# Second weights loaded in longer runs, features dealt to blocks in another way, order searched anew

## The chip, the cores and the metric

The kernel runs on one core of a Trainium2 chip. The metric is device microseconds of one execution; lower is better. Three executions of the kernel before took 1167.38, 1167.28 and 1159.86 us, with a median of 1167.28 us.

## The reference, cut to what matters

Two layers follow each other. The first is a causal weighted sum of seven neighbouring tokens, with weights from a softmax; its output is the input of the second, a layer of eight experts in which each token goes to one expert.

```python
w = softmax(weight_gen, axis=-1)                        # (8, 3584, 8 heads, 7 taps)
out[b, s, h, :] = sum_k w[b, s, h, k] * x_pad[b, s + k, h, :]   # x: (8, 3584, 192), heads of 24
x = out.reshape(28672, 192)

logits = x @ w_gate                                     # 8 experts
e_idx = argmax(logits); gate_w = softmax(logits)[e_idx]
eom = sigmoid(x @ w_output_gate)
for e in range(8):                                      # w1: (8, 192, 1024), w2: (8, 1024, 192)
    h = relu(x[mask] @ w1[e])
    out[mask] = gate_w * eom[:, e] * (h @ w2[e])
```

## The kernel before, in words

**The front** works on 32 units of 896 tokens (128 partitions by 7 tokens). For a unit, `load_steps` (line 655) loads `x` and the tap weights `w`, `softmax_steps` makes the weights, and `tap_steps` makes seven products of 128x1344. GpSimd makes some of them (the tile `gap`), VectorE the others; how many each makes for unit u is `TAPS(u)` (line 1409), from `PRO_G`, `FIRST_G`, `SHARES` and `POOL`. For the first `PE_U` = 6 units the sum of the seven products is made by TensorE: the first product is written to PSUM and the other six are added by float32 matmuls with the identity matrix `cf`, six instructions to a tap (`add_steps`, line 825). From unit 6 on VectorE adds them (`acc_steps`, line 775). `sum_steps` (line 850) scales a unit, splits it in two halves of float16 (the tile `rt`), and computes the router's logits. For these the unit is turned: for the first `TR_U` = 5 units by 21 TensorE transposes and 7 ScalarE copies to `gt`, afterwards by one transposing DMA on SP's queue (`gt<-rt`). `place_steps` (line 998) gives each token a row in the sorted tensor `srtd` in DRAM, and GpSimd scatters the rows with 7 indirect DMAs a unit (`srtd<-rt,posi`).

**The weights.** `weight_steps` (line 586) loads `w1` (4096- and 2048-byte runs) and `w2` of an expert into staging tiles `st1` and `st2`; four pairs of those exist. `split_steps` (line 603) takes the sum of squares (ScalarE, `sqd`), a scale, and writes each weight as two float16 halves: ScalarE writes the high half, VectorE the low one (`SCALAR_TENSOR_TENSOR`), into `wa` for `w1` and `wpb` for `w2`. Eight DMAs of an expert carry them back to the DRAM tensor `wd`. In `w2`'s load, partition p gets the eight rows p, 128+p, 256+p, ..., each a run of 768 bytes.

**The tiles.** As soon as enough rows are sorted, `plan_rounds` calls for tiles of 256, then 384, then 512 rows of one expert, at the end also of 128; there are 75 of them. `tile_steps` (line 1148) lets the first one go only when all eight experts are in `wd` (`state["weights"] == NE`), and `round_steps` only when the scatters of all units up to its own are issued; the first round is that of unit 2. `tile_load` (line 1170) reads the expert's number, the rows by a transposing DMA (`xT`), and both weights from `wd` (`wa<-wd`, `wb<-wd`), 1.6 MB a tile. `gemm1_unit` (line 1186) makes five matmuls to each block of 128 hidden features; ScalarE and VectorE evacuate them as two float16 halves (`hh`, `hl`). `gemm2_group` (line 1208) makes 24 matmuls of 192 columns to a group of 128 rows; ScalarE scales the result (`ys`), and GpSimd scatters it to the output.

**The order.** The program is written out by hand on all engines: generators ("chains") give up their turn at each `yield`, and `Order.step` always takes the one that its own estimate of times, a rank and a small favour put first. The estimate's constants, ranks, favours, shares and limits stand at the end of the file (from line 1415) and fix the order of the instructions on each engine. `stir` (line 502) puts dummy matmuls on TensorE where the estimate sees a gap (`STIR`). All DMAs but the scatters go out on SP's queue, in order. An instruction that a paced engine issues has line 207 in the profile; a DMA of SP's has line 175.

Of the kernel before, what the change touches and what calls it, by code (L numbers as in the profile page):

```python
# [14 lines left out]
ALU = mybir.AluOpType  # L15
AX = mybir.AxisListType.X

P = 128
# [138 lines left out]
class Queue:  # L157
# [12 lines left out]
    def __getattr__(self, name):  # L170
        f = getattr(self.engine, name)

        def call(*args, **kwargs):
# [6 lines left out]
            if own is not None:  # L180
# [3 lines left out]
                self.moved = max(self.moved, done)  # L184
                c.t = max(c.t, done + LANDED)
            return r
# [4 lines left out]
class Paced:  # L191


    def __init__(self, order, engine, cost, before=0.0, after=None, lead=0.0, follows=True, holds=None, first=None):
        self.order, self.engine, self.cost, self.t = order, engine, cost, 0.0
        self.before, self.after = before, LAT if after is None else after
        self.lead, self.follows, self.holds, self.first = lead, follows, holds, first
# [91 lines left out]
def sync_cost(name, args, kwargs):  # L289
    if not name.startswith("dma_start"):  # L290
        return None
    o = kwargs["out"]
    size = 4 if o.dtype in (F32, I32) else 2
    n = size
    for v in o.shape:
        n *= v
    if name == "dma_start_transpose":
        return n / 256 * 0.0185 / 16
    run = n // o.shape[0]
    if tuple(o.shape[1:]) == (8, 192):  # L300
        run = 768
    per = 0.009 if run <= 64 else 0.0265 + run / 6148 * 0.2145
    return n / run * per / 16

# [2 lines left out]
def kernel(ctx: ExitStack, tc: tile.TileContext, x, wg, wgate, wogate, w1, w2, cst, out):  # L307
    nc = tc.nc
    od = Order()
    V = Paced(od, nc.vector, vector_cost, holds=two_in_sbuf)  # L310
    S = Paced(od, nc.scalar, scalar_cost, after=LAT_S)
    G = Paced(od, nc.gpsimd, gpsimd_cost, holds=lambda kwargs: True)
    T_ = Paced(od, nc.tensor, tensor_cost, after=0.0, first=lambda gap: stir(gap))
    SP = Queue(od, nc.sync, sync_cost, sync_issue, LEAD)
    TQ = SP if TURN_SP else Queue(od, nc.scalar, sync_cost, sync_issue, LEAD, S)
    B, SEQ, D = x.shape
# [153 lines left out]
    o = 256  # L470
# [115 lines left out]
    def weight_steps(stg):  # L586

        for e in range(NE):
            yield from take(st_free, SP)

            st1 = stg.tile([P, 1536], F32, tag="st1", name=f"st1_{e}")
            st2 = stg.tile([P, 1536], F32, tag="st2", name=f"st2_{e}")
            SP.dma_start(out=st1[:, 0:1024], in_=w1[e, 0:128, :])
            for h in range(2):
                SP.dma_start(out=st1[64 * h : 64 * h + 64, 1024:1536], in_=w1[e, 128:192, 512 * h : 512 * h + 512])
            SP.dma_start(out=st2.rearrange("p (c d) -> p c d", d=D), in_=w2[e].rearrange("(c p) d -> p c d", p=P))
            od.add(split_steps(e, st1, st2), (RANK_W, e), S)
            if 3 < e < 7:

                scattered(SP.dma_start(out=srtd[DUMMY + (e - 3) * P : DUMMY + (e - 2) * P, :], in_=pad), -1)  # L600
            od.cur.t = od.now

    def split_steps(e, st1, st2):
        yield from take(sq_free, S)
        sqd = stg_sq.tile([P, 1536], BF16, tag="sqd", bufs=1, name=f"sqd{e}")
        ss = sp.tile([P, 2], F32, tag="wss", name=f"wss{e}")
        S.activation(sqd, st1, AF.Square, accum_out=ss[:, 0:1])
        yield S
        S.activation(sqd, st2, AF.Square, accum_out=ss[:, 1:2])
        sq_free.append(od.cur.t)  # L610
        yield from take(pg_free, T_)
        pg = ps[:, 1984:1986]
        T_.matmul(pg[:, 0:2], lhsT=ones32, rhs=ss, start=True, stop=True)
        yield V
        sc = sp.tile([P, 2], F32, tag="wsc", name=f"wsc{e}")
        inv = sp.tile([P, 2], F32, tag="winv", name=f"winv{e}")
        yield from scales(pg[:, 0:2], sc, inv, f"w{e}", pg_free)
        s1, s2 = sc[:, 0:1], sc[:, 1:2]
        _, wa = yield from take(wa_free, S)
        wah = wa.bitcast(F16)  # L620

        for lo, n in ((0, 1024), (2048, 512)):
            src = st1[:, lo // 2 : lo // 2 + n]
            hi = wah[:, lo : lo + n]
            yield S
            S.activation(hi, src, AF.Copy, scale=s1)
            yield V
            V.scalar_tensor_tensor(out=wah[:, lo + n : lo + 2 * n], in0=src, scalar=s1, in1=hi, op0=ALU.mult, op1=ALU.subtract)
        yield SP
        SP.dma_start(out=wd[e, :, 0:1024], in_=wa[:, 0:1024])  # L630
        for h in range(2):
            for q in range(2):
                SP.dma_start(out=wd[e, 64 * q : 64 * q + 64, 1024 + 256 * h : 1280 + 256 * h], in_=wa[64 * h : 64 * h + 64, 1024:1280])
            SP.dma_start(out=wd[e, 0:64, 1536 + 256 * h : 1792 + 256 * h], in_=wa[64 * h : 64 * h + 64, 1280:1536])
        wa_free.append((od.cur.t, wa))
        od.cur.t = od.now
        yield from take(wb_free, S)
        wb = wp.tile([P, WW - 2048], I32, tag="wb", bufs=WB, name=f"wpb{e}")
        wbh = wb.bitcast(F16)
        hi = wbh[:, 0:1536]  # L640
        yield S
        S.activation(wb.bitcast(F32)[:, 1536:1537], inv[:, 0:1], AF.Copy, scale=inv[:, 1:2])
        S.activation(hi, st2, AF.Copy, scale=s2)
        yield V
        V.scalar_tensor_tensor(out=wbh[:, 1536:3072], in0=st2, scalar=s2, in1=hi, op0=ALU.mult, op1=ALU.subtract)
        st_free.append(od.cur.t)
        yield SP
        SP.dma_start(out=wd[e, :, 2048:WW], in_=wb)
        wb_free.append((od.cur.t, "wb"))
        state["weights"] += 1  # L650
# [199 lines left out]
    def sum_steps(u):  # L850
# [40 lines left out]
        else:  # L891
            od.cur.t += LAT_T
            for j0 in range(0, JS, 2):
# [292 lines left out]
    def gemm1_unit(hp, d, u, at):  # L1186

        t, T, wa, xT = d["t"], d["T"], d["wa"], d["xT"]
        nf = 512 // T
        hh = hp.tile([P, 512], F16, tag="hh", name=f"hh{t}_{u}")  # L1190
        hl = hp.tile([P, 512], F16, tag="hl", name=f"hl{t}_{u}")
        for i in range(nf):
            f = u * nf + i
            b3 = 2048 + f * P
            for q, (wo, k) in enumerate(((f * P, 0), (1024 + f * P, 0), (f * P, 2), (b3, 1), (b3 + 1024, 1))):
                T_.matmul(ps[:, at + i * T : at + (i + 1) * T], lhsT=wa[:, wo : wo + P], rhs=xT[:, k, 0:T], start=(q == 0), stop=(q == 4), skip_group_check=True)
        od.add(evac_steps(d, ps[:, at : at + nf * T], hh[:, 0 : nf * T], hl[:, 0 : nf * T], at, u), (RANK_H,), S, T_.t + LAT_P)
# [10 lines left out]
    def gemm2_group(d, g, at):  # L1208
        t, T, wb = d["t"], d["T"], d["wb"]
        if g == 0:  # L1210
            d["ys"] = gp.tile([P, 4, D], F32, tag="ys", bufs=YB, name=f"ys{t}")
            d["sc"] = gp.tile([P, 4], F32, tag="sc", name=f"sc{t}")
        py = ps[:, at : at + D]
        nf = 512 // T
        for f in range(8):
            lo = (f % nf) * T + g * P
            hh = d["hh"][f // nf][:, lo : lo + P]
            hl = d["hl"][f // nf][:, lo : lo + P]
            w2h = wb[:, f * D : (f + 1) * D]
            w2l = wb[:, 1536 + f * D : 1536 + (f + 1) * D]  # L1220
            T_.matmul(py, lhsT=hh, rhs=w2h, start=(f == 0), stop=False)
            T_.matmul(py, lhsT=hh, rhs=w2l, start=False, stop=False)
            T_.matmul(py, lhsT=hl, rhs=w2h, start=False, stop=(f == 7))
        if g == d["G"] - 1:
            wb_free.append((T_.t + WBX, d["kb"]))
        od.add(out_steps(d, g, py, at), (RANK_Y,), S, T_.t + LAT_P)
# [122 lines left out]
    with tc.tile_pool(name="stg", bufs=STG, reuse_waits="tile") as stg:  # L1349
        stg_sq = stg  # L1350
        od.add(weight_steps(stg), (RANK_W, 0), SP)
        while state["weights"] < NE:
# [26 lines left out]
    with tc.For_i(0, left, 1):  # L1379
# [8 lines left out]
        d = tile_load(state["t"], P, ti, 0, ([], []), more, "wb")  # L1388
# [26 lines left out]
RANK_H, RANK_Y, RANK_C, RANK_R, RANK_B, RANK_A, RANK_G = 1, 0, 2, 3, 4, 5, 6  # L1415
HOLDS = {128: 768, 256: 1408, 384: 2304, 512: 2816}
TAILK = 79
RANK_W = 4.808
LAT = 0.076
LAT_S = 0.2324  # L1420
LAT_P = 0.384
LAT_T = 1.932
LOCK = True
ARRIVE = 1.9478
LANDED = 0.4
LAT_R = 0.851
SLACK = 0
SCATTER = 0.987
SMALL = 0.073
EAGER = 0, 0.2, (2, 3, 4)  # L1430
BACK = 0.899
W_LATE = 0
T_LATE = 0
TURNS = (1536,)
# [3 lines left out]
WB = 4  # L1438
HB = 16
AHEAD = 2  # L1440
DELAY = {128: 5, 256: 2, 384: 1, 512: 1}
LATE = 4
LATE_W = 4
XN = 3
# [3 lines left out]
MB = 8  # L1448
PRO_G = 4
POOL = (5, 5, 5, 4)  # L1450
SHARES = {11: 4, 28: 5, 20: 5, 2: 3, 4: 4, 29: 5, 6: 5, 23: 4, 1: 4, 27: 5, 0: 4, 30: 4, 18: 5, 14: 5, 26: 5, 19: 4, 15: 5, 25: 4, 31: 4, 22: 5, 3: 6}
FAVOUR = {'evac 1 0': 0.3, 'evac 72 6': 0.1, 'evac 1 4': -1.0, 'out 36 0': 0.8, 'evac 73 1': -0.5, 'out 33 1': 1.4}
PE_U = 6
STIR = (0.46, 0.31)
GIVE = 1
RANK_X = 2.767
X_EARLY = 4
RANK_GATE = 4.308
FIRST_G = (5, 4)
DEFER = 4  # L1460
WBX = 3.58
ROW = ()
PAIRS = 0
TURN_SP = True
GT = 1
TR_U = 5
EARLY = {2: ((256, 0),), 4: ((384, 0),), 5: ((384, 0),), 6: ((384, 0),), 3: ((384, 0),)}
EVERY = {*range(99)}
MANUAL = ("SP", "DVE", "PE", "Activation", "Pool")
# [18 lines left out]
```

## Time and profile before

| what | before |
|---|---|
| median of three executions | 1167.28 us |
| the profiled execution | 1169.75 us, of which the span is 1168.0 us |
| TensorE busy | 1096.7 us (94%) |
| VectorE busy | 939.9 us (80%) |
| GpSimd busy | 840.6 us (72%) |
| ScalarE busy | 620.9 us (53%) |
| mean granted TensorE clock | 0.973 |
| DMA packets | 294952, of which 229222 under 512 bytes |

The busy shares are means over two very different stages: until the first tile's matmuls (147.59 us) the kernel prepares weights and the first units, and from then to the end the tiles' matmuls run beside the front. Views by stretch tell the two apart.

### The profile page before, as it was taken

What the parts mean: (1) busy time and instruction counts of PE and PEld (TensorE: products, weight loads), DVE (VectorE), ACT (ScalarE), POOL (GpSimd) and SP (SyncE); (2) the same over time, 40 slices, a digit from 0 to 9 for tenths busy, and PEclk for the clock granted to TensorE, in tenths of its full rate; (3) what the DMA queues carried; (4) which work ended last, traced back from release to release, by engine and by line L of the source; (5) the groups of instructions that cost most, each with busy time, mean ns of one, the idle gap of its engine ahead of it and who ended that gap; (6) DMA issues with size and microseconds to landing.
All of it is one profiled execution on the core that took longest, in us unless ns stands there. A gap on an engine that the chain in (4) does not pass through costs nothing.

```text
span 1168.0 us, 26970 instructions
## 1 busy us (share of the span) xinstructions
PE 1096.7 (94%) x9622; PEld 804.3 (69%) x9622; DVE 939.9 (80%) x1874; ACT 620.9 (53%) x1300; POOL 840.6 (72%) x622
## 2 busy tenths in 40 slices
PE   8978588999999999999999999999999999999997
PEld 4544377777667766677667666767667777788897
DVE  6889879999999989888899999999999863333331
ACT  4986644566555545555555555555545544443442
POOL 7578775888788888788888898888888764322222
PEclk9988888999999999999999999999999999999999
DMA  9997899999996987979997897889958997699993
GB/s 291 275 309 247 247 271 316 280 273 262 249 242 157 246 192 209 250 213 244 230 232 205 255 273 196 237 216 250 254 155 224 231 256 233 189 293 273 299 320 90
DMA packets 294952, 282.77 MB, mean 242 GB/s; under 512 B 229222, under 2 KB 254423, under 8 KB 294816
## 3 DMA queue, kind: packets, MB, share of 16 engines
q1 hardware_dynamic: 272976, 236.54, 76.2%
q0 software_dynamic: 21696, 44.30, 12.5%
q8 instruction: 76, 1.25, 0.5%
q14 instruction: 60, 0.49, 0.1%
q10 hardware_dynamic: 144, 0.20, 0.1%
HBM read 174.77 MB, written 60.28 MB: 201 GB/s over the span
## 4 chain that ended last, share of the span: by engine, by line
PE 44%; DVE 26%; DMA 13%; issue 7%; POOL 6%; ACT 2%; SPq 1%; POOLq 0%; DVEq 0%; ACTq 0%
PE ps L207 44%; DVE ps L207 13%; DVE hl L207 6%; DMA gt<-rt 4%; POOL srtd L207 2%; POOL gap L207 2%; DMA wd<-wa 2%; DMA srtd<-rt,posi 2%; DVE rt L207 2%; DVE vt L207 2%; DMA wa<-wd 2%; POOL out_dram L207 1%; DMA w<-in_wg_dram 1%; SPq L175 1%; ACT rt L207 1%
## 5 line engine op out<-in xcount | busy, mean ns | idle before, releaser
L207 PE MATMUL ps<-xT,wa 128*128 128x512 f16 (+3 forms) x2480 | 503.0, 351 | 27.0 <-DMA wa<-wd 17.1
L207 PE MATMUL ps<-wb,hh 128*128 128x192 f16 x3648 | 473.5, 247 | 3.4 <-DVE hl L207 2.7
L207 PE MATMUL ps<-wb,hl 128*128 128x192 f16 x1824 | 451.0, 247 | 0.0
L207 DVE SCALAR_TENSOR_TENSOR hl<-ps,hh 128x512 f16<-128x512 f32 (+1 forms) x470 | 306.1, 664 | 143.8 <-ACT hh L207 143.4
L207 POOL TENSOR_TENSOR gap<-x,w 128x1344 f32<-128x1344 f32 x147 | 383.6, 2614 | 41.6 <-issue 10.9
L207 PEld LDWEIGHTS <-wa 128*128 128x128 f16 x2480 | 231.8, 99 | 215.8 <-issue 18.8
L207 ACT ACTIVATE hh<-ps 128x512 f16<-128x512 f32 (+1 forms) x470 | 270.5, 582 | 191.0 <-PE ps L207 188.2
L207 PEld LDWEIGHTS <-hh 128*128 128x128 f16 x3648 | 333.0, 98 | 45.0 <-issue 5.3
L207 POOL DMA_INDIRECT out_dram<-ys,meta x220 | 218.8, 995 | 187.3 <-ACT ys L207 141.0
L207 POOL DMA_INDIRECT srtd<-rt,posi x224 | 224.6, 1003 | 85.6 <-issue 60.7
L207 ACT ACTIVATE ys<-ps,sc 128x192 f32<-128x192 f32 x228 | 95.7, 420 | 223.6 <-PE ps L207 155.3
L207 DVE TENSOR_TENSOR ps<-ps,gap 128x1344 f32<-128x1344 f32 x123 | 191.0, 1553 | 3.7 <-POOL gap L207 3.6
L207 PEld LDWEIGHTS <-hl 128*128 128x128 f16 x1824 | 179.4, 98 | 0.1
L207 PE MATMUL ps<-gap,cf 128*128 128x512 f32 x144 | 64.9, 593 | 2.3 <-POOL gap L207 2.3
L207 DVE SCALAR_TENSOR_TENSOR rt<-ps,sx,rt 128x448 f16<-128x448 f32 x64 | 57.5, 909 | 9.5 <-ACT rt L207 7.7
L207 ACT ACTIVATE rt<-ps 128x1344 bf16<-128x1344 f32 x32 | 41.3, 1291 | 22.6 <-DVE ps L207 20.6
L207 ACT ACTIVATE rt<-ps,sx 128x1344 f16<-128x1344 f32 x32 | 44.1, 1377 | 14.7 <-DVE sx L207 14.0
L207 DVE TENSOR_TENSOR ps<-ps,vt 128x1344 f32<-128x1344 f32 x33 | 51.2, 1551 | 0.0
L207 DVE TENSOR_TENSOR vt<-x,ps 128x1344 f32<-128x1344 f32 x33 | 50.9, 1542 | 0.1
L207 DVE TENSOR_TENSOR ps<-x,ps 128x1344 f32<-128x1344 f32 x32 | 49.7, 1552 | 0.6 <-DVE ps L207 0.2
L207 PEld LDWEIGHTS ps<-gap,cf 128*128 128x128 f32 x144 | 27.9, 205 | 29.6 <-issue 25.8
L207 PEld LDWEIGHTS <-gt 128*128 128x128 f16 x672 | 24.3, 97 | 32.8 <-ACT gt L207 13.9
(123 smaller groups left out, 774.5 us busy)
## 6 DMA issues: line engine op xcount, KB each, us to landing
wb<-wd SPq DMA_DIRECT2D x75, 768.5 KB
wa<-wd SPq DMA_DIRECT2D x62, 768.0 KB
x<-in_x_dram SPq DMA_DIRECT2D x32, 672.0 KB
late<-wd SPq DMA_DIRECT2D x13, 768.0 KB
wa<-wd SPq DMA_DIRECT2D x62, 128.0 KB
w<-in_wg_dram SPq DMA_DIRECT2D x32, 196.0 KB
wd<-wpb SPq DMA_DIRECT2D x8, 768.5 KB
st<-in_w_dram SPq DMA_DIRECT2D x8, 768.0 KB
```

The lines of the kernel that those rows point to most:

```text
L175: r = f(*args, **kwargs)
L207: r = f(*args, **kwargs)
```

## The change

The second weights are loaded so that partition p gets, in each half of 512 rows, four neighbouring rows: two runs of 3072 bytes in place of eight of 768. Hidden feature 512h + 4p + c then stands in row p of block (h, c). So that the first product delivers the features in the same blocks, the columns of `w1` are read with a step of four elements when they are split (both ScalarE's and VectorE's read of `st1`); what is written stays contiguous. The two matmul functions index the blocks accordingly. The planner's price of the `w2` load is changed to the longer run. All other edits are constants that fix the order.

```diff
-    if tuple(o.shape[1:]) == (8, 192):
-        run = 768
+    if tuple(o.shape[1:]) == (2, 768):
+        run = 3072
...
-            SP.dma_start(out=st2.rearrange("p (c d) -> p c d", d=D), in_=w2[e].rearrange("(c p) d -> p c d", p=P))
+            SP.dma_start(out=st2.rearrange("p (h n) -> p h n", h=2), in_=w2[e].rearrange("(h p c) d -> p h (c d)", p=P, c=4))
...
-            src = st1[:, lo // 2 : lo // 2 + n]
-            hi = wah[:, lo : lo + n]
+            src = st1[:, lo // 2 : lo // 2 + n].rearrange("p (q c) -> p c q", c=4)
+            hi, low = (wah[:, at : at + n].rearrange("p (c q) -> p c q", c=4) for at in (lo, lo + n))
...
-            V.scalar_tensor_tensor(out=wah[:, lo + n : lo + 2 * n], in0=src, scalar=s1, in1=hi, op0=ALU.mult, op1=ALU.subtract)
+            V.scalar_tensor_tensor(out=low, in0=src, scalar=s1, in1=hi, op0=ALU.mult, op1=ALU.subtract)
...
-            b3 = 2048 + f * P
+            b3 = 2048 + (f % 2 * 4 + f // 2) * P
...
-            w2h = wb[:, f * D : (f + 1) * D]
-            w2l = wb[:, 1536 + f * D : 1536 + (f + 1) * D]
+            row = (f % 2 * 4 + f // 2) * D
+            w2h = wb[:, row : row + D]
+            w2l = wb[:, 1536 + row : 1536 + row + D]
...
-RANK_W = 4.808
+RANK_W = 4.243
...
-BACK = 0.899
+BACK = 1.0
...
-DELAY = {128: 5, 256: 2, 384: 1, 512: 1}
+DELAY = {128: 3, 256: 2, 384: 1, 512: 1}
...
-SHARES = {11: 4, 28: 5, 20: 5, 2: 3, 4: 4, 29: 5, 6: 5, 23: 4, 1: 4, 27: 5, 0: 4, 30: 4, 18: 5, 14: 5, 26: 5, 19: 4, 15: 5, 25: 4, 31: 4, 22: 5, 3: 6}
-FAVOUR = {'evac 1 0': 0.3, 'evac 72 6': 0.1, 'evac 1 4': -1.0, 'out 36 0': 0.8, 'evac 73 1': -0.5, 'out 33 1': 1.4}
-PE_U = 6
-STIR = (0.46, 0.31)
+SHARES = {11: 4, 28: 5, 20: 5, 29: 5, 6: 5, 23: 4, 1: 3, 24: 5, 9: 5, 18: 5, 26: 6, 3: 5, 19: 3, 15: 3, 31: 4, 25: 5, 7: 5, 21: 5, 5: 5, 27: 4, 2: 5, 10: 5}
+FAVOUR = {'place 7': 0.1, 'evac 33 0': 0.4, 'copy 0': -0.8, 'out 68 0': 0.3, 'evac 50 4': 1.4}
+PE_U = 7
+STIR = (1.17, 0.37)
 GIVE = 1
-RANK_X = 2.767
-X_EARLY = 4
-RANK_GATE = 4.308
-FIRST_G = (5, 4)
+RANK_X = 1.564
+X_EARLY = 3
+RANK_GATE = 3.529
+FIRST_G = (4, 4)
 DEFER = 4
-WBX = 3.58
-ROW = ()
+WBX = 2.799
+ROW = (6,)
...
-TR_U = 5
+TR_U = 4
```

Left out are small changes of the estimate's latencies (`LAT`, `LAT_S`, `LAT_T`, `LANDED`, `LAT_R`, `SLACK`). `RANK_W`, `RANK_X` and `RANK_GATE` rank the weights, the early loads (of units up to `X_EARLY`) and the gate's weights against other chains; `DELAY` is the distance between a tile's two products; `WBX` is when a weight buffer counts as free; `ROW` lets a unit's seven scatters go out in a row.

## Rows read from the trace of the kernel before

**Rows 1.** The page's first part: busy us, share, instructions.
```profile
PE 1096.7 (94%) x9622; PEld 804.3 (69%) x9622; DVE 939.9 (80%) x1874; ACT 620.9 (53%) x1300; POOL 840.6 (72%) x622
```
**Rows 2.** Stretches: length, busy us of PE, PEld, DVE, ACT, POOL, clock, DMA, GB/s.
```profile
30.00:60.00 30.00, 28.18 (x129) 15.09 (x127) 25.39 (x42) 28.54 (x46) 15.39 (x5) 1.00 0.93 271
60.00:90.00 30.00, 22.88 (x115) 12.30 (x116) 25.35 (x56) 24.84 (x45) 23.04 (x14) 0.79 0.96 314
120.00:150.00 30.00, 16.28 (x89) 8.71 (x88) 22.60 (x42) 15.52 (x30) 23.50 (x15) 0.76 0.83 237
150.00:180.00 30.00, 26.36 (x250) 22.95 (x249) 27.63 (x63) 15.61 (x35) 21.72 (x15) 0.84 1.04 273
180.00:210.00 30.00, 26.05 (x251) 22.18 (x249) 28.48 (x70) 16.16 (x40) 18.33 (x14) 0.89 1.12 325
...
300.00:400.00 100.00, 97.59 (x847) 69.29 (x846) 96.62 (x185) 54.70 (x117) 84.76 (x61) 1.00 0.89 218
...
900.00:1000.00 100.00, 100.00 (x859) 71.71 (x857) 61.52 (x148) 45.51 (x98) 60.05 (x60) 1.00 0.87 229
```
**Rows 3.** TensorE in order of time: start, length, instructions, idle before and its releaser.
```profile
147.59 2.31 PE L207 MATMUL ps<-xT,wa 128*128 128x256 f16 x10 [9.56 <-DMA wa<-wd]
...
152.63 1.26 PE L207 MATMUL ps<-xT,wa 128*128 128x256 f16 x10
...
174.09 4.45 PE L207 MATMUL ps<-xT,wa 128*128 128x256 f16 x20 [2.94 <-DMA wa<-wd]
...
198.23 3.38 PE L207 MATMUL ps<-xT,wa 128*128 128x384 f16 x10 [3.94 <-DMA wa<-wd]
```
**Rows 4.** SP's queue in order of time, around the first tile.
```profile
134.66 0.35 SPq L175 DMA_DIRECT2D wd<-wpb  x1
138.87 0.43 SPq L175 DMA_DIRECT2D meta<-srtd  x1
```
**Rows 5.** The chain of waits from 20 to 150 us: start, length, what.
```profile
131.37 7.17 DMA srtd<-rt,posi
...
141.17 6.37 DMA wa<-wd
```
**Rows 6.** DMA of SP's queue at 10:35, 60:80, 80:100, 100:120: packets, MB, share.
```profile
q1 hardware_dynamic: 5858, 7.60, 98.1%
...
q1 hardware_dynamic: 3245, 5.78, 89.8%
...
q1 hardware_dynamic: 3082, 4.45, 73.9%
...
q1 hardware_dynamic: 2271, 5.29, 74.5%
```
**Rows 7.** What SP's queue waited for from 10 to 160 us: total, times, longest.
```profile
SPq L175 <- DVE wpb L207: 9.5, 4, 5.7
SPq L175 <- DMA st<-in_w_dram: 9.4, 7, 2.2
```
**Rows 8.** Groups by form on VectorE and ScalarE: busy us, mean ns, idle before.
```profile
L207 DVE SCALAR_TENSOR_TENSOR wa<-st,wsc,wa 128x1024 f16<-128x1024 f32 x8 | 15.0, 1881 | 0.0
L207 DVE TENSOR_TENSOR lz<-p,ps 128x56 f32<-128x56 f16 x32 | 7.7, 242 | 1.0
L207 DVE TENSOR_TENSOR lz<-lz,ps 128x56 f32<-128x56 f32 x32 | 6.5, 202 | 0.3
L207 DVE SCALAR_TENSOR_TENSOR wa<-st,wsc,wa 128x512 f16<-128x512 f32 x8 | 6.2, 773 | 1.6 <-ACT wa L207 1.6
...
L207 ACT ACTIVATE wa<-st,wsc 128x1024 f16<-128x1024 f32 x8 | 9.2, 1146 | 1.9 <-DVE wsc L207 1.9
```
**Rows 9.** One tap's sum on TensorE, and VectorE's and GpSimd's groups by form.
```profile
102.33 2.42 PE L207 MATMUL ps<-gap,cf 128*128 128x512 f32 x6
...
L207 DVE TENSOR_TENSOR ps<-ps,gap 128x1344 f32<-128x1344 f32 x123 | 191.0, 1553 | 3.7 <-POOL gap L207 3.6
...
L207 POOL TENSOR_TENSOR gap<-x,w 128x1344 f32<-128x1344 f32 x147 | 383.6, 2614 | 41.6 <-issue 10.9 <-DVE fm L207 10.0 <-DVE w L207 5.4
```
**Rows 10.** The tile gt (ns min/median/max, first and last start), and VectorE's end of unit 4.
```profile
L207 ACT COPY gt<-ps x35: 451/479/495, 39.1 to 153.0; 128x384 f16<-128x384 f16 x35
L175 SPq DMA_TRANSPOSE gt<-rt x27: 4119/6806/11013, 154.7 to 931.2; - x27
...
129.10 1.15 DVE L207 SCALAR_TENSOR_TENSOR rt<-ps,sx,rt 128x896 f16<-128x896 f32 x1
```

More of the change, by code (lines that the diff above doesn't have):

```diff
@@ L1417 @@
 TAILK = 79
-RANK_W = 4.808
-LAT = 0.076
-LAT_S = 0.2324
+RANK_W = 4.243
+LAT = 0.07
+LAT_S = 0.224
 LAT_P = 0.384
-LAT_T = 1.932
+LAT_T = 1.85
 LOCK = True
 ARRIVE = 1.9478
-LANDED = 0.4
-LAT_R = 0.851
-SLACK = 0
+LANDED = 0.449
+LAT_R = 0.739
+SLACK = 0.031
 SCATTER = 0.987
```

## The prediction

> **What bounds the kernel now.** The page's first part comes first: TensorE is busy for 94% of the span, every other engine less [rows 1]. The view by stretches shows that this mean covers two stages [rows 2]. From 300 us on TensorE is busy 97.6 us of 100, and 100 of 100 near the end, while VectorE has 38 us free there; in that stage only TensorE's work or its waits count. Before about 210 us it is otherwise: between 120 and 150 us TensorE works 16.28 us of 30 at a mean clock of 0.76. So the end is, to a good approximation, the moment of the first tile's matmul plus TensorE's work after it, and what moves that moment moves the end.
>
> TensorE in order of time gives the moment: the first tile starts at 147.59 us after 9.56 us idle, ended by the weights' load `wa<-wd` [rows 3]. SP's queue and the chain of waits say what that load waited for [rows 4, 5]. Two conditions come true almost together. The last expert's store goes out at 134.66 us. The last of unit 2's scatters starts at 131.37 us and lands 7.17 us later, at 138.54, and the first `meta` load follows at 138.87. Then the load itself takes 6.37 us. An earlier end of the weights alone gains nothing here unless the scatters come earlier too; both share the DMA rings, whose share is 0.93 and 0.96 between 30 and 90 us [rows 2].
>
> **The change part by part.** *The load of w2.* An expert's load falls from 128 x 8 = 1024 runs to 256, so 8 x 768 = 6144 packets go. I solve "share x length x 16 = packets x a + MB x b" for two pairs of stretches [rows 6]. 10:35 (392 us of DMA engine time) with 60:80 (287 us) gives a = 9 ns a packet. 80:100 (236 us) with 100:120 (238 us) gives 31 ns. Over 16 engines 6144 packets then cost 3.5 to 11.9 us of ring time. I take 3.5: four of the eight loads lie in 10:35, 4096 of its 5858 packets. The queue waited 9.4 us in all for loads into `st` [rows 7], so so much can lie on the path. Term: -3.5, from -11.9 to 0 (the other wait of that size, 9.5 us for VectorE's `wpb`, stays). [...]
>
> *The split of w1.* It has as many instructions as before, but ScalarE and VectorE now read `st1` at a step of 16 bytes, 1536 elements an expert on each, 12288 in all. No row shows a float32 read at that step. The nearest pair is VectorE's two subtractions and additions into `lz` over 56 elements: 202 ns where the read is in runs of eight, 242 ns where `p` is read at a step of 14 bytes, 0.71 ns an element more [rows 8]. That bounds the price: nothing, or 12288 x 0.71 = 8.7 us on VectorE and, if ScalarE is hit likewise, 8.7 us more there, 17.4 if both stood in series on the path; below nothing is excluded, as no element less is read. VectorE's splits of w1 now take 15.0 + 6.2 us [rows 8], on an engine busy about 25 of 30 us in this stage [rows 2], so most of it would show, but beside DMA waits. I take +1.5, an eighth of the way, because the pair differs in type as well as in step.
>
> *Unit 6 summed on TensorE (PE_U 7).* Six taps of 2.42 us [rows 9] put 14.5 us on TensorE. Cover is the 9.56 us in front of the first tile, and the idle 3.6 + 4.0 us from 150 to 210 [rows 2, 3]. If both covers hold the term is -1; if unit 6's taps come late, it is +14.5. VectorE loses six additions and gains one product, 5 x 1.55 = 7.8 us, in a stage where it is busy 27.6 of 30 us. [...] I take +1: 14.5 less 9.56, less 2.1, less some of the idle; ends -3 and +14.5.
>
> *Unit 4 turned by DMA (TR_U 4).* Seven copies of 0.48 us leave ScalarE and 21 transposes TensorE, where both have room. One transposing DMA comes onto SP's queue, and holds it for 4.1 to 11.0 us [rows 10]. The unit is split at 130.25 us [rows 10], so it can go ahead of the last weight store or of the first tile's `meta`, `xT`, `wa` and `wb`, all behind it in order. The queue's 3.9 us of rest between 135.0 and 138.87 [rows 4] hide the shortest one; the longest leaves 7.1 us. I take 0, ends 0 and +7.1.
>
> *Shares.* Counted from the lists, GpSimd makes 144 products instead of 147 (3 x 2.61 us less), VectorE 230 products and additions instead of 233 (3 x 1.55 less, the eight of unit 6 becoming three among them) [rows 9]. Cost nothing: after 210 us TensorE covers both. If that cover went, 1 us per unit could show in units 15 and 19, where VectorE gets two and one products more.
>
> *The rest of the order.* `X_EARLY`, ranks, latencies, `STIR`, `DELAY` and `WBX` change when things go out, not what. No row prices that. What it can win is the waits for tile weights at 174 and 198 us, 2.94 + 3.94 us [rows 3], and the second half of TensorE's slow stretches around them (clock 0.84 and 0.89 of 30 us each: 4.8 + 3.3 us) [rows 2]: 15 us. It can lose as much by new ones. I take -2, for the loads behind which those waits arise share rings with less queued ahead; ends -15 and +15. The index edits in the two products alter no count: 0.
>
> **Sum.** -3.5 + 1.5 + 1 + 0 + 0 - 2 = -3.0 on the profiled execution's 1169.75 us, 1166.75. That execution stands 2.5 us above the median of the runs, so the median would come to 1164.3; I say 1164.
>
> **The rivals.** *Everything arrives early.* The packet price is the upper one (-11.9, another 8.4) and the waits at 174 and 198 us largely go (another 5 of the 15): 1164 - 13 = 1151. For it: the second pair of stretches, and that both gates of the first tile hang on the rings. Against: the scatters of unit 2 wait for GpSimd and VectorE, not for the weights' loads. Chance 0.23.
>
> *The strided read sets the pace, slower.* Place: the splits of w1. Price: 8.7 us (VectorE alone) to 17.4 us. It decides when the last store moves past 138.5 us, that is with more than 4 us of it on the path; then it takes the gain of the load, and the time is 1167 + 8.7 - 3 = 1173 to 1181. For it: rows 8, and VectorE and ScalarE busy 25 and 28 us of 30 [rows 2]. Against: the pair's other differences, and slack in a chain that waits for DMA. [...] Chance 0.13.
>
> *TensorE's start is blocked.* The turning DMA goes ahead of the first tile's loads (+7.1) or unit 6's sums come after them (+13.5 beyond the forecast): 1171 to 1178. For it: the transposes' maximum of 11.0 us [rows 10]. Against: it needs an order that puts them there. Chance 0.10.
>
> *The longer runs change nothing*: the load's landing is set by what is queued ahead, and the new order is worth nothing: 1166 to 1168. Chance 0.06.
>
> **How the numbers follow.** The forecast has 0.48. Its own range, with the order's term at a third of its ends, is 1156 to 1173. A measurement of this kernel can tell about 1% from no change, 11.7 us: the bounds are 1155.6 and 1179. Faster by over that: the first rival (0.21 of 0.23) and the low tail of the forecast (0.06), 0.27. Slower: the upper part of the second rival and of the third, and their sum (0.07 + 0.05), and a bad order (0.02), 0.14. Same: 0.59. The range 1148 to 1179 leaves out about one in ten on each side.
>
> **What would show each step.** Load: fewer packets by 6144, and less than 9 us of the queue's waits for `st`. Split: `wa<-st` of 1024 elements over 1.15 us on ScalarE, or well over its mean of 1.88 on VectorE. First tile: its matmul before 147.59 us; each microsecond there should appear at the end. Unit 6: 36 more float32 matmuls, and whether they stand before or after the first tile. Unit 4: the first `gt<-rt`, and what SP issues behind it. Order: idle at the second and fourth tile. The prediction is wrong if the end moves by much more or less than the first tile's start does, or if TensorE falls under 95% busy after 300 us.

## The result, and the profile after

The changed kernel took 1176.91 us (median of five runs, 1169.71 to 1185.76) beside 1162.73 us for the kernel before (five runs, 1159.86 to 1167.38): a ratio of 1.0104, 95% interval 1.0066 to 1.0141. It is slower, by about 12 us by the ratio. Its profiled execution took 1185.76 us (span 1184.0), the slowest of the five, so the two profiles lie 16 us apart where the medians lie 14.2 apart.

The page's first part answers to [rows 1]:

```profile
PE 1111.9 (94%) x9660; PEld 810.8 (68%) x9660; DVE 948.6 (80%) x1871; ACT 631.7 (53%) x1293; POOL 836.9 (71%) x619
```

TensorE's share is the same. Its sum is 15.2 us longer, about the 14.5 us that the prediction gave unit 6's float32 sums; the other engines' sums moved by 4 to 11 us. That extra work alone can't be the loss: of the experiments below, e1 and e2 have the same extra work and lie 0.2% above the kernel before, e6 has none of it and lies 0.75% above. The view by stretches (length, busy us of PE, PEld, DVE, ACT, POOL, clock, DMA share, GB/s) says where the time went; it answers to [rows 2]:

```profile
30.00:60.00 30.00, 26.26 (x100) 13.25 (x99) 27.60 (x27) 27.35 (x35) 18.43 (x6) 1.00 0.88 268
60.00:90.00 30.00, 23.21 (x115) 12.17 (x115) 24.92 (x47) 26.96 (x42) 14.71 (x8) 0.87 0.92 295
...
120.00:150.00 30.00, 23.82 (x107) 11.99 (x108) 27.03 (x55) 12.29 (x28) 23.77 (x15) 0.78 0.72 205
150.00:180.00 30.00, 20.56 (x116) 12.49 (x114) 15.77 (x45) 10.52 (x21) 26.87 (x18) 0.91 1.02 236
180.00:210.00 30.00, 28.07 (x292) 25.70 (x293) 28.28 (x59) 16.22 (x37) 16.93 (x11) 0.92 0.93 270
...
300.00:400.00 100.00, 98.71 (x864) 70.78 (x863) 96.87 (x201) 58.34 (x123) 88.10 (x60) 1.00 0.87 227
...
900.00:1000.00 100.00, 99.73 (x858) 71.32 (x857) 69.34 (x174) 47.95 (x104) 66.84 (x63) 1.00 0.95 252
```

From 300 us on TensorE is as full as before. Between 150 and 180 us it now runs 116 matmuls where it ran 250, and VectorE is busy 15.77 us where it was 27.63. So the loss lies ahead of 300 us. TensorE in order of time answers to [rows 3] (start, length, idle before and its releaser):

```profile
159.74 1.51 PE L207 MATMUL ps<-xT,wa 128*128 128x256 f16 x10 [2.10 <-DMA wa<-wd]
161.05 6.22 PE L207 MATMUL ps<-gap,cf 128*128 128x512 f32 x12
167.10 1.25 PE L207 MATMUL ps<-xT,wa 128*128 128x256 f16 x10
...
179.01 0.72 PE L207 MATMUL ps<-gm,gt 128*128 128x32 f16 x21 [5.33 <-DVE hl L207]
181.54 6.01 PE L207 MATMUL ps<-xT,wa 128*128 128x256 f16 x40 [1.81 <-issue]
```

The first tile starts 12.15 us later than before, 159.74 against 147.59. Behind it stand unit 6's float32 sums and waits for `hl`; how much of the other 4 us of the two profiles they make isn't shown. SP's queue answers to [rows 4]:

```profile
130.11 0.34 SPq L175 DMA_DIRECT2D wd<-wpb  x1
137.50 5.02 SPq L175 DMA_TRANSPOSE gt<-rt  x1
...
151.01 0.43 SPq L175 DMA_DIRECT2D meta<-srtd  x1
```

The last weight store goes out 4.5 us *earlier* than before, and the first `meta` load 12.1 us later. The chain of waits, to be read beside [rows 5], names the other gate, unit 2's scatters, whose last one starts at 145.10 us where it started at 131.37:

```profile
145.10 5.58 DMA srtd<-rt,posi
...
153.04 6.66 DMA wa<-wd
```

What held the scatters is on GpSimd: what it waited for from 50 to 150 us (total, times, longest), first of the changed kernel, then of the kernel before.

```profile
POOL srtd L207 <- ACT rt L207: 16.5, 4, 9.3
POOL gap L207 <- ACT rt L207: 14.2, 1, 14.2
```
```profile
POOL gap L207 <- DVE fm L207: 10.0, 1, 10.0
...
POOL srtd L207 <- ACT rt L207: 1.9, 1, 1.9
```

GpSimd now waits 30.7 us for ScalarE's write of `rt`, before 1.9. This pair of kernels can't tell how much of that is the new order's and how much the strided read's; e1 below can. ScalarE has one reason to be late; the groups by form (busy us, mean ns, idle before) answer to [rows 8]:

```profile
L207 DVE SCALAR_TENSOR_TENSOR wa<-st,wsc,wa 128x1024 f16<-128x1024 f32 x8 | 21.2, 2650 | 2.8 <-ACT wa L207 2.8
...
L207 ACT ACTIVATE wa<-st,wsc 128x1024 f16<-128x1024 f32 x8 | 17.1, 2140 | 0.0
...
L207 DVE SCALAR_TENSOR_TENSOR wa<-st,wsc,wa 128x512 f16<-128x512 f32 x8 | 12.0, 1497 | 1.9 <-DMA srtd<-pad 1.2 <-ACT wa L207 0.7
...
L207 ACT ACTIVATE wa<-st,wsc 128x512 f16<-128x512 f32 x8 | 9.8, 1226 | 0.0
```

ScalarE's split of 1024 elements takes 2140 ns for 1146, the one of 512 takes 1226 (721 before): 8 x (0.994 + 0.505) = 12.0 us more. VectorE's two groups take 33.2 us for 21.2, in another order of instructions (e1 parts the two causes).

### The profile page after: what moved, and what is told of

Same layout as the page of the kernel before. It is cut to its first block, busy times and chain, and to the rows that moved or that the text cites. A ratio compares the mean times of both kernels' runs of the same rounds, so it can differ in the third digit from the quotient of the medians.

```text
span 1184.0 us, 27042 instructions
## 1 busy us (share of the span) xinstructions
PE 1111.9 (94%) x9660; PEld 810.8 (68%) x9660; DVE 948.6 (80%) x1871; ACT 631.7 (53%) x1293; POOL 836.9 (71%) x619
## 3 DMA queue, kind: packets, MB, share of 16 engines
q8 instruction: 76, 1.25, 0.5%
## 4 chain that ended last, share of the span: by engine, by line
PE 48%; DVE 19%; DMA 16%; issue 7%; POOL 5%; ACT 3%; SPq 1%; POOLq 0%; DVEq 0%; ACTq 0%
PE ps L207 48%; DVE ps L207 9%; DMA gt<-rt 7%; DVE hl L207 4%; DMA srtd<-rt,posi 3%; POOL gap L207 2%; DMA w<-in_wg_dram 2%; DMA wa<-wd 2%; SPq L175 1%; POOL out_dram L207 1%; DVE rt L207 1%; ACT wa L207 1%; DVE wa L207 1%; POOL srtd L207 1%; DMA meta<-srtd 1%
## 5 line engine op out<-in xcount | busy, mean ns | idle before, releaser
L207 PE MATMUL ps<-xT,wa 128*128 128x512 f16 (+3 forms) x2440 | 480.8, 346 | 15.3 <-DVE hl L207 8.7
L207 POOL TENSOR_TENSOR gap<-x,w 128x1344 f32<-128x1344 f32 x144 | 377.4, 2626 | 30.1 <-ACT rt L207 14.2
L207 PEld LDWEIGHTS <-wa 128*128 128x128 f16 x2440 | 225.3, 98 | 192.0 <-issue 21.9
L207 POOL DMA_INDIRECT srtd<-rt,posi x224 | 227.1, 1014 | 99.0 <-issue 59.4
L207 DVE TENSOR_TENSOR ps<-ps,gap 128x1344 f32<-128x1344 f32 x116 | 180.1, 1552 | 1.5 <-POOL gap L207 1.2
L207 PE MATMUL ps<-gap,cf 128*128 128x512 f32 x168 | 75.9, 597 | 1.3 <-DVE ps L207 0.9
L207 PE MATMUL ps<-xT,late 128*128 128x128 f16 (+2 forms) x560 | 59.9, 263 | 3.3 <-DMA late<-wd 3.3
L207 PEld LDWEIGHTS ps<-gap,cf 128*128 128x128 f32 x168 | 33.3, 209 | 34.5 <-issue 31.9
L207 PE MATMUL ps<-gm,gt 128*128 128x32 f16 x672 | 26.1, 178 | 28.6 <-ACT gt L207 13.3
L207 PEld LDWEIGHTS <-late 128*128 128x128 f16 x560 | 40.0, 98 | 16.3 <-DMA late<-wd 3.9
```

What stands on the lines that cost most here:

```text
L207: r = f(*args, **kwargs)
```

## The experiments

Two theories were set against each other. Theory S: the read of w1 at a step of 16 bytes, which the planner does not know of, makes ScalarE and VectorE late in the first stage. Theory O: the new order is worse whatever the split takes. Each group of up to four kernels has its own runs of the kernel before, whose median was 1200.54 us (e1 to e4), 1158.63 (e5 to e8), 1199.37 (e9 to e12) and 1205.44 (e13 to e16); why these differ by 4% is open. Times are therefore compared within a group, by the ratio to the kernel before, or between two kernels of one group. The first tile's start is from one profile of each kernel: two profiles of the kernel before give 147.59 and 145.25 us (e8), two of the changed kernel 159.74 and 157.13 (e5), so differences of 2 to 3 us between groups say nothing. "Old order" is the order of the kernel before, instruction for instruction.

| kernel | order | load | read of w1 | ratio, 95% interval | first tile, us |
|---|---|---|---|---|---|
| e1 | new | 3072 | plain | 1.0023 (1.0004 to 1.0042) | 151.03 |
| e2 | new | 768 | plain | 1.0022 (0.9999 to 1.0045) | 149.57 |
| e3 | old | 3072 | plain | 0.9982 (0.9961 to 1.0004) | 148.17 |
| e4 | old | 768 | 16 bytes | 1.0052 (1.0036 to 1.0068) | 156.03 |
| e5 | new | 3072 | 16 bytes | 1.0098 (1.0075 to 1.0121) | 157.13 |
| e6 | old | 3072 | 16 bytes | 1.0075 (1.0053 to 1.0097) | 153.35 |
| e7 | old | 1536 | 8 bytes | 1.0021 (0.9997 to 1.0045) | 144.77 |
| e8 | old | 768 | plain (kernel before) | one run, 1160.85 us | 145.25 |
| e9 | old | 3072 | 16 bytes, ScalarE only | 1.0033 (1.0001 to 1.0066) | 153.23 |
| e10 | old | 3072 | 16 bytes, VectorE only | 1.0017 (0.9996 to 1.0038) | 149.96 |
| e11 | old | 3072 | plain; matmul steps 8 bytes | 1.0004 (0.9984 to 1.0023) | 147.81 |
| e12 | new | 1536 | 8 bytes | 1.0026 (0.9999 to 1.0053) | 148.19 |

**e1, the changed kernel with a plain read of w1.**

```diff
-            src = st1[:, lo // 2 : lo // 2 + n].rearrange("p (q c) -> p c q", c=4)
+            src = st1[:, lo // 2 : lo // 2 + n].rearrange("p (c q) -> p c q", c=4)
```

> The changed kernel with w1 read contiguously when it is split; load of w2 and order stay as changed. The hidden features of the two products then do not match, so its result is not the layer's. Theory S (the strided read makes the first tile late): ScalarE's 1024-element split falls from 2.14 to 1.15 us, the first tile starts 8 to 14 us before 159.74, and the time falls by 10 to 15 us, to the time of the kernel before or under it. Theory O (the new order puts unit 2's scatters late whatever the split takes): the first tile stays within 4 us of 159.74 and the time within 5 us of the changed kernel's.

Measured: 1.0023, the first tile at 151.03, 8.7 us before 159.74. By the first tile that is Theory S. The time came down to a quarter of a per cent above the kernel before, not under it, so something of the order's own is left. GpSimd's waits for `rt` from 50 to 150 us, in the view that was shown above for the changed kernel, are:

```profile
POOL srtd L207 <- ACT rt L207: 18.5, 4, 8.1
POOL gap L207 <- ACT rt L207: 9.1, 1, 9.1
```

That is 27.6 us without any strided read. So nearly all of the step from 1.9 to 30.7 us belongs to the new order, and the total of these waits is no measure of what the read costs. Its delay shows instruction by instruction on GpSimd, in the same order in both kernels (start, length, wait and its releaser), first e1, then the changed kernel:

```profile
57.24 10.57 POOL L207 TENSOR_TENSOR gap<-x,w 128x1344 f32<-128x1344 f32 x4 [9.07 <-ACT rt L207]
75.88 1.16 POOL L207 DMA_INDIRECT srtd<-rt,posi  x1 [8.06 <-ACT rt L207]
...
136.33 1.01 POOL L207 DMA_INDIRECT srtd<-rt,posi  x1 [0.17 <-issue]
```
```profile
65.13 10.83 POOL L207 TENSOR_TENSOR gap<-x,w 128x1344 f32<-128x1344 f32 x4 [14.18 <-ACT rt L207]
85.21 1.16 POOL L207 DMA_INDIRECT srtd<-rt,posi  x1 [9.25 <-ACT rt L207]
...
145.10 1.01 POOL L207 DMA_INDIRECT srtd<-rt,posi  x1 [0.17 <-issue]
```

The first scatter of all is 9.3 us later in the changed kernel, 6.3 of it in these two waits, and unit 2's last scatter 8.8 us, the shift of the first tile. Of the 13.7 us by which that last scatter moved against the kernel before, about 5 are the order's. With a plain read in the new order ScalarE's two groups take 9.1 + 5.7 us and VectorE's 13.1 + 9.6: the read alone costs 12.1 and 10.5 us of busy time.

**e2, the kernel before with the new constants.**

```diff
     if tuple(o.shape[1:]) == (8, 192):
-        run = 768
+        run = 3072
...
-PE_U = 6
+PE_U = 7
...
```

> The kernel before with the new constants alone (the planner given the price of the longer run, so that the order is that of the changed kernel): loads of 768 bytes, contiguous split. Theory S: 1155 to 1165 us beside about 1163 for the kernel before, since without the strided read the new order is at worst equal. Theory O: 1170 to 1180. Against e1 it gives what the longer runs are worth in the new order: by the price of 9 ns a packet 3.5 us less ring time in e1, by 31 ns 11.9.

Measured: 1.0022, under Theory O's 1170 to 1180 by its ratio (1165.3 on 1162.73) and at the upper end of Theory S's. Against e1 the two medians are 1203.38 and 1202.12 us: the longer runs are worth 1.3 us in the new order, less than the runs can tell from nothing.

**e3 and e4, the old order with one half of the edit each.** e3 has the new load, which is shown, with a plain read; e4 has the old load with the strided read of the change.

```diff
-            SP.dma_start(out=st2.rearrange("p (c d) -> p c d", d=D), in_=w2[e].rearrange("(c p) d -> p c d", p=P))
+            SP.dma_start(out=st2.rearrange("p (h n) -> p h n", h=2), in_=w2[e].rearrange("(h p c) d -> p h (c d)", p=P, c=4))
...
```

> The kernel before, its order kept, with the w2 load in 3072-byte runs alone (contiguous split, so the hidden features of the two products do not match). Theory S and O alike: 0 to 4 us under the kernel before, because unit 2's scatters hold the first tile as well as the weights; if the runs of 768 bytes were what held the first stage, 4 to 12 us under it.

> The kernel before, its order kept, with the 16-byte step in the read of w1 alone (old load, so the hidden features of the two products do not match). Theory S: ScalarE and VectorE gain 12 us of busy time each in the first stage, the first tile starts 8 to 14 us after 147.59, and the time is 8 to 14 us over the kernel before. Theory O: within 4 us of the kernel before.

Measured: e3 0.9982, 2.2 us under the kernel before by the ratio, with an interval that just reaches 1. e4 1.0052, 6.2 us over it, with the first tile 7.9 us after e3's. That is Theory S for the first tile; at the end 6 us were seen, a little under the 8 to 14 expected. Between 10 and 160 us SP's queue waited for `st` and for VectorE's `wpb` as follows, in e3 and then in e4:

```profile
SPq L175 <- DVE wpb L207: 16.2, 3, 6.9
...
SPq L175 <- DMA st<-in_w_dram: 4.0, 4, 1.5
```
```profile
SPq L175 <- DVE wpb L207: 21.4, 4, 8.5
...
SPq L175 <- DMA st<-in_w_dram: 3.8, 3, 1.9
```

These rows answer to [rows 7]. With the strided read the queue waits 5.2 us more for VectorE's splits than in e3.

**e5 to e8, the changed kernel again, the pair in the old order, a step of 8 bytes, and a profile of the kernel before.** e6 is the changed code with the old constants. e7 differs from e6 in loading two neighbouring rows of w2 to a run of 1536 bytes, so that w1 is read at a step of 8 bytes:

```diff
-            SP.dma_start(out=st2.rearrange("p (h n) -> p h n", h=2), in_=w2[e].rearrange("(h p c) d -> p h (c d)", p=P, c=4))
+            SP.dma_start(out=st2.rearrange("p (h n) -> p h n", h=4), in_=w2[e].rearrange("(h p c) d -> p h (c d)", p=P, c=2))
...
-            src = st1[:, lo // 2 : lo // 2 + n].rearrange("p (q c) -> p c q", c=4)
+            src = st1[:, lo // 2 : lo // 2 + n].rearrange("p (q c) -> p c q", c=2)
...
```

> The changed kernel itself, on the chip of the experiments. If parts simply add, its ratio is that of e1 (1.0023) times what the strided read costs: in the old order 1.0052, which gives 1.0075; if the new order suffers more from the stride (its first tile came 8.7 us later than e1's), 1.009 to 1.011, as measured first.

> The kernel before, its order kept, with the longer load and the strided read that belongs to it; its result is the layer's. Theory S with parts that add: 1.0052 times 0.9982, 1.0034, the first tile at 154 to 156 us. If the new order is what costs most, this is within 0.2% of the kernel before; if the longer load made up for the stride, it is under 1.0.

> [...] If the price of the stride comes with a step of 16 bytes and not of 8: ScalarE's 1024-element split is back at 1.15 us, the first tile at 147 to 149 us, the ratio 0.997 to 1.000. If any step costs: ScalarE near 2.1 us and the ratio as in e6.

> The kernel before, unchanged, for a profile on the chip of the experiments. All theories: first tile at 147 to 149 us, ScalarE's 1024-element split 1.15 us.

Measured: e5 1.0098, as first measured. e6 1.0075, the first tile at 153.35, 8.1 us after e8's; by the ratio 8.7 us at the end, so in this group the end followed the first tile one for one. That is more than the 1.0034 expected from e3 and e4 if parts add; the read was worth 6.2 us at the end there (e4) and 8.7 together with the longer load here, and why the groups differ is open. e8's first tile lies before the 147 to 149 expected. The chain of waits of e6 runs through both engines' splits to unit 2's scatters and from there to the first tile's weights:

```profile
108.49 2.15 ACT wa L207
...
110.66 4.11 DVE wa L207
...
139.89 5.77 DMA srtd<-rt,posi
...
148.30 5.01 DMA wa<-wd
```

e7 has 1.0021, the first tile at 144.77. The two splits on ScalarE, first in e6, then in e7:

```profile
L207 ACT ACTIVATE wa<-st,wsc 128x1024 f16<-128x1024 f32 x8 | 17.2, 2146 | 1.7 <-DVE wsc L207 1.7
L207 ACT ACTIVATE wa<-st,wsc 128x512 f16<-128x512 f32 x8 | 9.8, 1229 | 0.0
```
```profile
L207 ACT ACTIVATE wa<-st,wsc 128x1024 f16<-128x1024 f32 x8 | 9.8, 1225 | 1.8 <-DVE wsc L207 1.7
...
L207 ACT ACTIVATE wa<-st,wsc 128x512 f16<-128x512 f32 x8 | 6.1, 767 | 0.0
```

At 8 bytes 1024 elements cost 79 ns more than a plain read (1146 in e8), at 16 bytes 1000 ns. The order of instructions is the same in both. e7's ratio is a little over the 1.000 expected for it, its interval begins just under 1; with the first tile back, 8.6 us before e6's, the price of the step is settled, the last 0.2% is not.

**e9 and e10, the step on one engine alone.** As e6, with `flat`, a contiguous view of the same columns, for the other engine:

```diff
+            flat = st1[:, lo // 2 : lo // 2 + n].rearrange("p (c q) -> p c q", c=4)
...
-            V.scalar_tensor_tensor(out=low, in0=src, scalar=s1, in1=hi, op0=ALU.mult, op1=ALU.subtract)
+            V.scalar_tensor_tensor(out=low, in0=flat, scalar=s1, in1=hi, op0=ALU.mult, op1=ALU.subtract)
```

e10 is the other way round: `flat` on ScalarE, the step on VectorE.

> The kernel of e6 with the 16-byte step left in ScalarE's read of w1 alone; VectorE reads contiguously, so high and low halves do not belong together. If ScalarE's price (about 12 us of busy time) is what delays the first tile, its start is 151 to 154 us and the ratio 1.004 to 1.008; if VectorE's is, 145 to 148 us and 0.997 to 1.002.

> The kernel of e6 with the 16-byte step left in VectorE's read alone; ScalarE reads contiguously, so high and low halves do not belong together. If VectorE's price delays the first tile: 151 to 154 us and 1.004 to 1.008; if ScalarE's does: 145 to 148 us and 0.997 to 1.002. If both stand in series on the path, e9 and e10 show about half of e6's delay each.

Measured: with e11 (no step in the split) at 147.81 in the same group, ScalarE's step alone moves the first tile by 5.4 us, VectorE's by 2.2. By the ratio 4.0 and 2.0 us reach the end; VectorE's interval takes in 1, and ScalarE's 1.0033 is under the 1.004 to 1.008 expected. So ScalarE's step is the larger part. The two delays nearly add to e6's 8.1, but that VectorE's alone delays anything isn't clear of noise. VectorE's price, undisturbed by the other's, stands in e10:

```profile
L207 DVE SCALAR_TENSOR_TENSOR wa<-st,wsc,wa 128x1024 f16<-128x1024 f32 x8 | 21.1, 2638 | 0.0
L207 DVE SCALAR_TENSOR_TENSOR wa<-st,wsc,wa 128x512 f16<-128x512 f32 x8 | 9.2, 1154 | 0.4 <-ACT wa L207 0.4
```

2638 for 1882 and 1154 for 776 ns (e11) are 0.74 ns an element, 9.1 us in all. VectorE's times depend on the order too: at the step of 8 bytes the same two splits take 1873 and 775 ns in the old order (e7), 1599 and 1173 ns in the new one (e12).

**e11, the step moved to the matmuls' weights.** The split is plain as before, and the first product reads every fourth column:

```diff
-                T_.matmul(ps[:, at + i * T : at + (i + 1) * T], lhsT=wa[:, wo : wo + P], rhs=xT[:, k, 0:T], start=(q == 0), stop=(q == 4), skip_group_check=True)
+                T_.matmul(ps[:, at + i * T : at + (i + 1) * T], lhsT=wa[:, wo : wo + 4 * P - 3 : 4], rhs=xT[:, k, 0:T], start=(q == 0), stop=(q == 4), skip_group_check=True)
...
```

> The kernel before, its order kept, with the w2 load in 3072-byte runs, the split of w1 contiguous as before, and the step moved to the weights that the first product's matmuls read: every fourth float16, 8 bytes apart. Its result is the layer's. If the weight load does not mind the step: first tile at 144 to 147 us, LDWEIGHTS of wa 98 ns as before, ratio 0.996 to 1.000. If it minds: LDWEIGHTS near 190 ns in 2480 instructions; hidden under 512-column matmuls (215 ns), not under those of 128 and 256, some 10 to 30 us more.

Measured: 1.0004, the first tile at 147.81, both just above what was expected, and the weight loads 115 ns for 99, between the two values expected. Of the figures in that expectation, 190 ns was seen on float32 weight loads alone (`ps<-vap,cf`, 72 in the kernel before), and 512-column matmuls do come about 215 ns apart (there ten, of 379 ns each, take 2.32 us from 607.29). The loads in e9, which reads these weights plainly, and then in e11:

```profile
L207 PEld LDWEIGHTS <-wa 128*128 128x128 f16 x2480 | 231.8, 99 | 235.5 <-issue 47.4 <-DMA wa<-wd 11.1
```
```profile
L207 PEld LDWEIGHTS <-wa 128*128 128x128 f16 x2480 | 263.7, 115 | 208.3 <-issue 46.5 <-DMA wa<-wd 12.8
```

16 ns a load add 32 us to the busy sum of these 2480 loads and show nowhere in the time. So the longer runs can be had without the price; they are worth nothing that can be measured here.

**e12, the changed kernel at a step of 8 bytes**, edited as e7.

> The changed kernel, its order kept, with runs of 1536 bytes and a step of 8 bytes. Its result is the layer's. Theory S: the stride's price is gone, the first tile starts near 149 to 151 us and the ratio is that of e1 and e2, 1.001 to 1.004; what is left over 1.0 is the new order's own. If the order alone made the loss: 1.008 to 1.011.

Measured: 1.0026, the first tile at 148.19: halving the step takes the price away in the new order too, and what is left is the value of e1 and e2. From 148 to 180 us, with the first tile at the same moment, the stretch in e3 and then in e12:

```profile
148.00:180.00 32.00, 28.23 (x262) 24.24 (x263) 27.75 (x64) 15.82 (x35) 26.04 (x17) 0.82 1.08 260
```
```profile
148.00:180.00 32.00, 21.14 (x161) 15.82 (x162) 18.15 (x31) 9.37 (x19) 29.08 (x19) 0.84 1.13 285
```

TensorE does 161 matmuls for 262 in that stretch. Which setting does that was the next question.

**e13 to e16, the two large settings undone and done alone**, the planner ordering anew around each. e13 and e14 start from e2, e15 and e16 from the kernel before.

```diff
# e13: PE_U = 6, FIRST_G = (5, 4), SHARES 15: 4 and 19: 4
# e14: TR_U = 5
# e15: PE_U = 7, FIRST_G = (4, 4)
# e16: TR_U = 4
```

> The kernel of e2 (new constants, short runs, contiguous read) with PE_U back at 6 and FIRST_G at (5, 4), and 4 products instead of 3 on GpSimd in units 15 and 19, which the buffers want then; the planner orders anew around it. If unit 6's sums behind the first tile make the order's loss: 0.997 to 1.001, with 1150 or more tile matmuls by 300 us less what this condition of the chip costs, that is at least 60 more than e2's 1009. If not: 1.002 to 1.005.

> The kernel of e2 with TR_U back at 5: unit 4 turned by TensorE again. If the turning DMA on SP's queue makes the order's loss: 0.997 to 1.001, and the tiles after the second start 5 to 10 us earlier than in e2. If unit 6's sums do: 1.002 to 1.004.

> The kernel before with PE_U 7 and FIRST_G (4, 4) alone; the planner orders anew around it. If unit 6 on TensorE costs: 1.002 to 1.006, float32 matmuls behind the first tile's and 60 to 100 tile matmuls fewer by 300 us. If not: 0.998 to 1.001.

> The kernel before with TR_U 4 alone. If the turning DMA costs: 1.002 to 1.006 (4 to 7 us on the path by the prediction's bound). If not: 0.998 to 1.001.

Measured: 1.0109 (1.0075 to 1.0143), 1.0063 (1.0041 to 1.0084), 1.0094 (1.0063 to 1.0125) and 1.0040 (1.0019 to 1.0061). Each of the four is slower than the order that it starts from, whether it brings the setting or takes it back; both theories on the settings fall. The first tile starts at 149.34, 152.63, 158.86 and 155.90 us. A setting that is moved alone, with the other constants left where they were, costs 0.4 to 0.9% against the order that it starts from, more than the two whole orders differ. So these runs can't say which setting makes the 0.2%; that stays open.

## Why the prediction was wrong, point by point

The time lies in the range, but the prediction said a little faster and the kernel is 1% slower. The step that failed is the term for the split of w1: "I take +1.5, an eighth of the way, because the pair differs in type as well as in step." Both halves of that failed. The price: VectorE's is 0.74 ns an element (e10), and the row of `lz<-p` [rows 8] had given 0.71; ScalarE's is 0.97 (994 ns in 1024), above what was called the upper bound, so that 21 us of busy time came on (12.0 on ScalarE, 9.1 on VectorE), not 17.4 at most. And the share on the path: 1.5 is a twelfth of 17.4, not the eighth that was written, and the runs show 8.1 us at the first tile in the old order (e6 against e8) and 6.2 (e4) to 8.7 us (e6) at the end. The "slack in a chain that waits for DMA" was not there: the order on each engine is fixed, and in the changed kernel both are busy 25 to 28 of each 30 us from 30 to 90 us.

The rival on the strided read had the right cause, and its 1173 to 1181 us holds the result; it was given 0.13. Its place was half right. In the old order the last store goes from 134.23 (e8) to 143.17 us (e6), as it said. But there too unit 2's scatters are the later gate: the last one lands at 145.66 in e6, and `meta` starts at 145.99 (137.50 and 137.84 in e8). In the changed kernel the last store comes early and the scatters alone are late, by the 8.8 us that e1 shows. That the first tile has two gates was read correctly; that late splits delay the second was not followed through.

*The load.* Packets of 512 bytes and more fell from 65730 to 59586, by 6144 as counted. The price of about 9 ns holds: the stretch 10:35 of the changed kernel answers to the first line of [rows 6].

```profile
q1 hardware_dynamic: 3457, 8.14, 99.0%
```

Solved with that first line of before it gives 8.6 ns. The gain on the path was 2.2 us in the old order (e3) and 1.3 in the new one (e1 against e2), neither clear of zero, where 3.5 was taken: the sign may be right, the size was that of ring time, and the scatters gate the first tile too. The sign that was named for it, under 9 us of the queue's waits for `st`, came in e3 (4.0 us) and not in the changed kernel (10.6 from 10 to 170 us).

*Unit 6 on TensorE.* 36 more float32 matmuls, of which the last 12 stand behind the first tile (161.05 us), as feared. No run shows the 2.1 us that the sum takes off. In their place: the first tile's ten matmuls take 1.51 us where they took 2.31 (granted clock 0.87 from 159.70 to 161.10, before 0.50 from 147.50 to 150.00), and the next ten 1.25 where they took 2.34; but between the two stand the 12 float32 matmuls, 6.22 us at a granted clock of 0.74. What the term is by itself could not be separated (e13, e15); together with the rest of the new order it came to 0.2%, 2.6 us (e2).

*Unit 4 by DMA.* The transposing DMA holds the queue for 5.02 us from 137.50, between the last weight store and the first `meta` at 151.01, which waits for the scatters; no cost to the first tile in the changed kernel, as taken.

*The order.* -2 was taken for it, -1 with the terms of units 6 and 4, which these runs can't part from it; it is +0.2% without the strided read (e1, e2, e12, three values with the same sign, intervals that reach down to 1.0004, 0.9999 and 0.9999). The read costs about the same in both orders: e2's 1.0022 times e6's 1.0075 gives 1.0097, and e5, with both, has 1.0098. So by these runs some three quarters of the loss are the read's and a quarter the order's; with e4's 1.0052 for the read alone it would be a half.

*The end against the first tile.* The first tile moved by 12.15 us, the profiled span by 16.0, but that profile is of the slowest of five executions; by the ratio the end moved by 12.1, and by 11.4 for 11.9 in the group of e5 and e8. So the forecast that the end follows the first tile holds for the change as a whole. For the order alone it doesn't: e12's first tile stands where e11's does, at 148.19 for 147.81, its medians are 2.5 us apart, and between 148 and 180 us its tiles are slower than e3's.

## What to carry to other kernels

A layout that saves packets on one side can be paid for in the read on the other: price the stepped read on every engine that makes it, and give a reason for any share of it that is taken to be hidden: here 6 to 9 of 21 us reached the end. When an instruction gets longer on an engine whose order is fixed, follow what is queued behind it to every gate of the next stage, not only to its own product. The settings of a searched order belong together: each of four that was moved alone made this kernel 0.4 to 0.9% slower.

## What the runs showed of the hardware that was not expected

Reading w1's float32 at a step of 16 bytes cost ScalarE 0.97 ns an element on top of a plain read (2140 for 1146 ns in 1024 elements, the changed kernel and the kernel before) and VectorE 0.74 (2638 for 1882 and 1154 for 776 ns, e10 and e11). At 8 bytes ScalarE paid 0.08 (1225 ns in e7, 1146 in e8) and VectorE nothing that shows (1873 and 1882). A weight load of float16 at a step of 8 bytes took 115 ns (e11) where a plain one took 99 (e9).
